# Masked pairs of v and r: one VectorE operation in place of a ScalarE copy and two GpSimd selections

## The chip, the cores and the metric

The kernel runs on one core of a Trainium2 chip. A core has a matrix engine (TensorE, in the profile PE, its weight loads PEld), a vector engine (VectorE, DVE), a scalar engine (ScalarE, ACT) and a general engine (GpSimd, POOL). DMA queues are fed by the sync engine (SP) and by ACT. Matmul results land in PSUM, eight banks of 2 KB per partition; everything else lives in SBUF. The metric is the device time of one execution in microseconds; lower is better. Before the change the median of three timed runs is 599.76 us (597.77 to 600.04).

## The reference

A recurrent attention with a 40 x 40 state per head (4 batches, 8 heads, 768 steps), followed by a small MoE-like product on its output. In short:

```python
# r, k, v, w, a, b: (4, 8, 768, 40) float32
for t in range(S):
    y[:, :, t] = einsum('bhd,bhde->bhe', rt, state)
    Sa = einsum('bhde,bhe->bhd', state, at)
    state = state * wt[:, :, None, :] - einsum('bhd,bhe->bhde', Sa, bt) \
            + einsum('bhd,bhe->bhde', vt, kt)
x = y.transpose(0, 2, 1, 3).reshape(B * S, H * D)      # (3072, 320)
a = x @ w1; b = x @ w2                                 # w1, w2: (320, 1024)
out = ((a * b) @ w3) @ w_out                           # w3: (1024, 1024), w_out: (1024, 320)
```

The weights of the MoE part arrive as 8-byte floats.

## The kernel before

**Tiling.** The 768 steps are cut into 12 chunks of 64 (C = 64). Inside a chunk the recurrence becomes matrix work: the steps of a chunk act on each other through a strictly triangular 64 x 64 matrix per head, which is inverted, and the state is carried from chunk to chunk. The eight heads of a batch are four pairs (NP = 4); the two heads of a pair sit in the two halves of the 128 partitions. Two batches are done together, so a chunk has two such groups.

**Stages of one chunk**, by the tags of the code: `ld` loads decay (fm), k and b (xx) and a (aa); `sc` scans the decay and scales aa and xx with it; `ca` forms the causal products (PSUM to JP and lm, lm masked by POOL); `so` inverts the triangular blocks in many small DVE operations (multiply into tmp, reduce, in lines 681 and 685); `jo` joins the blocks; `pa` forms the pair products of v and r; `tk` transposes xx into bk; `rec` (tags `r.`) runs the recurrence of the chunk on PE, with DVE masking (un, line 922) and ACT copies (un, hs, SB) between the products; `ga` gathers y into xr by DMA; `m.` is the MoE part: xs (xr split in a high and a low part, lines 972 and 975), products with w1 and w2 (line 988), a * b (ga, line 1001), its split in gh and gl (gl in line 1004), the output product (line 1013) and the store. w3 and w_out are multiplied once at the start (line 540) after their conversion from 8-byte floats (`cv`, lines 443 to 461), piece by piece through four raw buffers. A check of the weights (`ck`, lines 484 to 496) reads them a second time along the way.

**The pairs.** For each chunk and batch, `pa.mm` (line 822) writes a 128 x 256 product into a PSUM bank. An ACT copy `pa.cp` (line 827) brings it into vg, columns 0 to 63 of each pair; then two POOL selections `pa.mask` (line 831), one for each half of the partitions, set to zero what is not strictly above the diagonal. The other 40 columns of each pair come by DMA (`pa.v`). The recurrence reads vg in `r.zv` and in two more products. This is done 48 times (12 chunks x 4 batches).

**What sets the order.** Every step is recorded as an operation with a tag, its reads and its writes. The table RANK gives each operation a number, and the whole program is written out in the order of these numbers; each engine works through its operations in that order. The table ON says for seven kinds of operation, one letter per instance, which engine does it (d DVE, p POOL, a ACT). Buffers are handed out in the same order: a slot is free again when its last reader has been written out. One rule concerns DVE and POOL: DVE operations whose tag is in the set TWO are noted, and a POOL operation is given a dependence on the last noted one ahead of it in the program. The pair copies, as well as the other operations that read PSUM (un, y, st, a * b), are not in that set.

**The mask.** mask_h is made at the start: -1 where the column is greater than the row of its half, 0 elsewhere in the first 64 columns, and -1 in the other 40. The masking of un multiplies a PSUM bank with it.

## Time and profile before

| | |
|---|---|
| median of 3 timed runs | 599.76 us |
| profiled execution | 603.52 us |
| its span, first to last instruction | 601.8 us |
| PE busy | 544.7 us, 91% |
| DVE busy | 496.2 us, 82% |
| ACT busy | 411.9 us, 68% |
| POOL busy | 149.1 us, 25% |
| mean granted PE clock | 0.978 |

A busy time is a union over the engine's instructions, as a share of the span. Idle time of PE is what its instructions waited for others. The profiled execution is a single one; its time is compared with its own span, and the median stands for the kernel.

### The profile page before, as it was taken

The numbers are of one execution on the slowest core, as the hardware profiler recorded it, in microseconds if no ns is written. First come the engines' busy times: TensorE is split into PE (matmuls) and PEld (weight loads), VectorE is DVE, ScalarE is ACT, GpSimd is POOL, SyncE is SP. The second block draws the span as 40 slices with busy tenths as digits, with TensorE's granted clock in tenths as the row PEclk, the third lists the DMA queues.
The fourth block names the chain that finished last, engine by engine and source line by source line (L and its number), as shares of the span: only waits on it lengthen the run. The fifth ranks groups of instructions, "written<-read, shape, count | busy, mean of one in ns | idle before, by whom it ended". The sixth has DMA issues, their size and how long they took to land.

```text
span 601.8 us, 26711 instructions
## 1 busy us (share of the span) xinstructions
PE 544.7 (91%) x11714; PEld 491.4 (82%) x11714; DVE 496.2 (82%) x955; ACT 411.9 (68%) x888; POOL 149.1 (25%) x218
## 2 busy tenths in 40 slices
PE   1197998899999999999999899999999999999994
PEld 1175676799888898899898798998988998998994
DVE  5998899899699797995797896995997998956672
ACT  7888859954947649548639549567576497377562
POOL 3013242112411324034322133233121330151000
PEclk9997999799999999999999999998998999999998
DMA  8988785442235053533252535334452445337671
GB/s 249 295 274 261 223 244 144 114 126 52 77 100 151 18 146 90 136 85 98 52 165 62 132 83 148 98 80 127 131 137 90 145 123 167 107 96 225 225 242 30
DMA packets 56812, 83.45 MB, mean 139 GB/s; under 512 B 30320, under 2 KB 38000, under 8 KB 56688
## 3 DMA queue, kind: packets, MB, share of 16 engines
q1 hardware_dynamic: 56300, 81.34, 47.8%
q8 instruction: 94, 1.54, 1.1%
q10 hardware_dynamic: 388, 0.33, 0.2%
q14 instruction: 30, 0.25, 0.1%
HBM read 72.99 MB, written 3.93 MB: 128 GB/s over the span
## 4 chain that ended last, share of the span: by engine, by line
PE 56%; DVE 21%; ACT 12%; issue 5%; DMA 4%; SPq 1%; ACTq 0%; POOL 0%; DVEq 0%
PE bank L988 24%; PE bank L871 15%; PE bank L1013 9%; DVE tmp L681 4%; ACT JP L330 3%; PE bank L629 3%; ACT TT L330 2%; DVE TDX L657 2%; PE bank L846 2%; DMA fm<-in_fmg_dram 2%; PE bank L822 1%; PE bank L783 1%; DVE Tp L685 1%; DVE un L922 1%; DVE TDX L685 1%
## 5 line engine op out<-in xcount | busy, mean ns | idle before, releaser
L988 PE MATMUL bank<-xs,W 128*128 128x256 f32 x1536 | 208.4, 288 | 1.2 <-ACT ga L330 0.6
L988 PEld LDWEIGHTS bank<-xs,W 128*128 128x128 f32 x1536 | 189.8, 190 | 9.1 <-issue 1.5
L1004 POOL TENSOR_TENSOR gl<-ga,gh 128x512 fp32r<-128x512 f32 x30 | 38.6, 1288 | 145.1 <-DVE tmp L681 49.8
L831 POOL TENSOR_SCALAR_AFFINE_SELECT vg<-vg 64x256 f32<-64x256 f32 x96 | 42.4, 448 | 117.8 <-DVE tmp L681 48.5
L1013 PE MATMUL bank<-W3h,gh 128*128 128x320 f32 x192 | 62.3, 324 | 0.0
L1013 PE MATMUL bank<-W3h,gl 128*128 128x320 f32 x192 | 59.6, 310 | 0.6 <-POOL gl L1004 0.6
L1013 PE MATMUL bank<-W3l,gh 128*128 128x320 f32 x192 | 59.3, 309 | 0.0
L330 ACT ACTIVATE ga<-bank 128x512 f32<-128x512 f32 x48 | 28.4, 597 | 42.4 <-PE bank L988 42.2
L645 POOL TENSOR_SCALAR_AFFINE_SELECT lm<-lm 64x512 f32<-64x512 f32 x48 | 33.4, 701 | 86.9 <-DVE tmp L681 30.4
L871 PE MATMUL bank<-un,bk 64*64 64x104 f32 (+1 forms) x768 | 46.2, 258 | 5.6 <-DVE un L922 5.5
L330 ACT ACTIVATE JP<-bank 64x256 f32<-64x256 f32 (+2 forms) x120 | 45.2, 378 | 7.1 <-PE bank L629 4.7
L871 PE MATMUL bank<-hs,TT 64*64 64x104 f32 x768 | 47.1, 263 | 1.3 <-ACT TT L330 1.2
L330 ACT ACTIVATE gh<-ga 128x512 fp32r<-128x512 f32 x48 | 30.3, 631 | 25.5 <-DVE ga L1001 22.7
L871 PEld LDWEIGHTS bank<-un,bk 64*64 64x64 f32 (+1 forms) x768 | 36.4, 126 | 12.3 <-DVE un L922 8.5
L1001 DVE TENSOR_TENSOR ga<-bank,ga 128x512 f32<-128x512 f32 x48 | 32.9, 686 | 15.7 <-ACT ga L330 7.9
L871 PE MATMUL bank<-vg,bk 64*40 64x104 f32 (+1 forms) x768 | 44.9, 256 | 0.7 <-issue 0.7
L846 PE MATMUL bank<-ident,xx 104*128 104x104 f32 x192 | 27.4, 273 | 18.3 <-DVE xx L601 18.3
L922 DVE TENSOR_TENSOR un<-bank,mask_h 128x416 f32<-128x416 f32 x48 | 28.2, 587 | 18.4 <-PE bank L871 16.4
L629 PE MATMUL bank<-aa,xx 40*64 40x64 f32 x1536 | 32.2, 237 | 10.5 <-DVE aa L590 7.3
L871 PEld LDWEIGHTS bank<-hs,TT 64*64 64x64 f32 x768 | 37.2, 138 | 4.7 <-ACT TT L330 1.7
L540 PE MATMUL bank<-wof,w3f 128*128 128x320 f32 x128 | 40.6, 471 | 0.0
L629 PEld LDWEIGHTS bank<-aa,xx 40*64 40x64 f32 x1536 | 29.1, 150 | 14.0 <-issue 10.5
(127 smaller groups left out, 1265.0 us busy)
## 6 DMA issues: line engine op xcount, KB each, us to landing
rv<-in_rv_dram SPq DMA_DIRECT2D x24, 588.0 KB
xx<-in_fmx_dram SPq DMA_DIRECT2D x24, 448.0 KB
raw<-in_w3t_dram SPq DMA_DIRECT2D x16, 512.0 KB
JP<-in_w3t_dram SPq DMA_DIRECT2D x11, 512.0 KB
fm<-in_fmg_dram SPq DMA_DIRECT2D x24, 227.5 KB
aa<-in_fma_dram SPq DMA_DIRECT2D x24, 224.0 KB
raw<-in_w_dram SPq DMA_DIRECT2D x10, 512.0 KB
vg<-in_vt_dram SPq DMA_DIRECT2D x48, 80.0 KB
```

Of the source, the lines that this page charges most:

```text
L330: act.activation(out_, in_, AF.Copy, scale=scale)
L540: pe.matmul(out=pt.t[:, 0:DM], lhsT=w[:, j], rhs=wof[:, j], start=(j == 0), stop=(j == NJ - 1))
L629: pe.matmul(out=bank(s)[64 * z:64 * z + 64, i, p], lhsT=X[r, p, z], rhs=aa.t[r, i, p], start=True, stop=True)
L645: op("ca.mask", lambda q=q: pool.affine_select(out=lm.t[q], in_=lm.t[q], pattern=[[0, 2 * NP], [1, C]], compare_op=ALU.is_gt, fill=0.0, ba ...
L831: op("pa.mask", lambda q=q, vg=vg: pool.affine_select(out=vg.t[q, :, 0:C], in_=vg.t[q, :, 0:C], pattern=[[0, NP], [1, C]], compare_op=ALU. ...
L846: pe.transpose(out=bank()[:, p], in_=X[:, p].rearrange("q x t -> q (x t)"), identity=ident[0:104, 0:104])
L871: pe.matmul(out=out_(ab ^ z, p), lhsT=left(ab, ab ^ x, p), rhs=right(ab ^ x, p), start=start and p == 0, stop=True, skip_group_check=True)
L922: dve.tensor_tensor(out=un[i].t, in0=view(hp[i]), in1=mask_h.unsqueeze(1).to_broadcast([128, NP, N]), op=ALU.mult)
L988: pe.matmul(out=pt.t[:, TOK * x:TOK * x + TOK], lhsT=WT[k][:, cs], rhs=xs.t[:, z], start=(n == 0), stop=(n == 7))
L1001: op("m.ab", lambda a=a, pt=pt: dve.tensor_tensor(out=a.t, in0=wide(pt), in1=a.t, op=ALU.mult), r=[pt], w=[a])
L1004: both("m.gl", lambda e, a=a, j=j: e.tensor_tensor(out=gl.t[:, j:j + 2], in0=a.t, in1=gh.t[:, j:j + 2], op=ALU.subtract), r=[a, (gh, j)], ...
L1013: pe.matmul(out=pt.t[:, 0:DM], lhsT=l.t[:, j, ts], rhs=W3[r][:, j], start=(j == 0 and n == 0), stop=(j == NJ - 1 and n == 2))
```

## The change

The pair products leave PSUM in one DVE operation: out = (PSUM * -1) * mask_h. Since the mask holds -1 and 0, this is the copy and the selection at once, for all 128 partitions. The ACT copy and the two POOL selections go. All tables of the order (RANK) and of the engines (ON) are replaced. In ON the count of DVE instances changes for gl (18 to 8 of 48), aa (15 to 13 of 24), xx (20 to 16 of 24), the conversion sums cv.add (26 to 23 of 31) and the check's squarings ck.sq (18 to 13 of 31); in the first four the rest is on POOL, in the last on ACT. Line numbers behind the tables move by 4, and behind the edited lines by 8.

```diff
 OPS = {
...
-    "act": "... jo.cp1 jo.cp2 jo.tt pa.cp tk.cp r.n "
+    "act": "... jo.cp1 jo.cp2 jo.tt tk.cp r.n "
-    "dve": "cv.t cv.add/d ...
+    "dve": "pa.cp cv.t cv.add/d ...
-    "pool": "w.lo/p cv.add/p sc.aa/p sc.xs/p ca.mask pa.mask m.gl/p",
+    "pool": "w.lo/p cv.add/p sc.aa/p sc.xs/p ca.mask m.gl/p",
...
 ON = {
-    "cv.sign": "aadaaddaadadaaaaddaaaaaadaadaaa",
-    "cv.add": "dddddddpdddddddddddpdpddddpdpdd",
-    "w.lo": "dddpddpddddp",
-    "sc.aa": "ddddddddpdpppddppdpdpdpd",
-    "sc.xs": "ddddddpddddddppdddpddddd",
-    "m.gl": "ddddppppppdpdpdpdpppddpppdpdpppdpppdpppppppdddpd",
-    "ck.sq": "ddaaaaaaddddaddadddaadaadddddda",
+    "cv.sign": "aaaaadadaaddaaaadaaaaaadddaaada",
+    "cv.add": "dpdddddddpdddddddddppppdpdpdddd",
+    "w.lo": "ddppdddddpdd",
+    "sc.aa": "ddpdpdpppdddpdpdpdppdddp",
+    "sc.xs": "ddddpdpppdddpdpdddpdpddd",
+    "m.gl": "pddppppdpppppppppppppppppdpppppppppppppppdppdpdd",
+    "ck.sq": "ddaaddaadaaaaadaadadaddaadaadad",
 }
...
-    "pa.cp": "135 140 211 216 333 348 416 403 638 627 697 708 ...
+    "pa.cp": "250 267 277 275 321 325 421 445 643 623 699 698 ...
...
         for vg, pt in zip(vgs, pts):
-            op("pa.cp", lambda vg=vg, pt=pt: copy(vg.t[:, :, 0:C], bank(pt)[:, :, 0:C]), r=[pt],
-               w=[(vg, 0), (vg, 1)])
-            for ab in range(2):
-                q = slice(64 * ab, 64 * ab + 64)
-                op("pa.mask", lambda q=q, vg=vg: pool.affine_select(
-                    out=vg.t[q, :, 0:C], in_=vg.t[q, :, 0:C], pattern=[[0, NP], [1, C]], compare_op=ALU.is_gt, fill=0.0,
-                    base=0, channel_multiplier=-1), w=[(vg, ab)])
+            op("pa.cp", lambda vg=vg, pt=pt: dve.scalar_tensor_tensor(
+                out=vg.t[:, :, 0:C], in0=bank(pt)[:, :, 0:C], scalar=-1.0,
+                in1=mask_h[:, 0:C].unsqueeze(1).to_broadcast([128, NP, C]), op0=ALU.mult, op1=ALU.mult), r=[pt], w=[(vg, 0), (vg, 1)])
```

On DVE, ahead of the inversion of the second chunk (the transposition of JP into TDX), the order before reads as follows; ISA is a sum of the weight conversion (line 461).

```order
105 L461 ISA mf_170<-mf_170,rs_169 128x1024
106 L461 ISA w3f_177<-w3f_177,rs_168 128x1024
107 L447 TENSOR_SCALAR mf_171<-raw_164 128x512
108 L657 STREAM_TRANSPOSE TDX_121<-JP_145 128x32x32
109 L681 TENSOR_TENSOR tmp<-DG,TDX_121 128x4
```

At the same place the order now holds the first chunk's four evacuations of the pairs (line 823), between conversion steps:

```order
103 L457 ISA w3f_177<-w3f_177,rs_168 128x1024
104 L450 TENSOR_SCALAR rs_168<-raw_163 128x512
105 L443 TENSOR_SCALAR mf_170<-raw_163 128x512
106 L823 SCALAR_TENSOR_TENSOR vg_126<-bank_153,mask_h 128x4x64
107 L457 ISA mf_170<-mf_170,rs_168 128x1024
108 L823 SCALAR_TENSOR_TENSOR vg_127<-bank_155,mask_h 128x4x64
109 L823 SCALAR_TENSOR_TENSOR vg_124<-bank_157,mask_h 128x4x64
110 L653 STREAM_TRANSPOSE TDX_121<-JP_145 128x32x32
111 L677 TENSOR_TENSOR tmp<-DG,TDX_121 128x4
```

Three of the four are seen here, the fourth stands a few rows further up. On POOL, in the same early part of the program, the order before reads (line 831 is a selection on vg, line 645 one on lm, line 461 a conversion sum):

```order
35 L645 AFFINE_SELECT lm_118<-lm_118 64x512
36 L831 AFFINE_SELECT vg_127<-vg_127 64x4x64
37 L831 AFFINE_SELECT vg_126<-vg_126 64x4x64
38 L645 AFFINE_SELECT lm_117<-lm_117 64x512
39 L461 TENSOR_TENSOR w3f_177<-w3f_177,rs_168 128x512
40 L461 TENSOR_TENSOR w3f_178<-w3f_178,rs_169 128x512
41 L461 TENSOR_TENSOR mf_170<-mf_170,rs_168 128x512
```

And now:

```order
31 L641 AFFINE_SELECT lm_117<-lm_117 64x512
32 L457 TENSOR_TENSOR w3f_179<-w3f_179,rs_169 128x512
33 L641 AFFINE_SELECT lm_118<-lm_118 64x512
34 L457 TENSOR_TENSOR w3f_178<-w3f_178,rs_168 128x512
35 L457 TENSOR_TENSOR w3f_177<-w3f_177,rs_169 128x512
36 L524 TENSOR_TENSOR W_2_103<-mf_171,W_0_102 128x512
37 L457 TENSOR_TENSOR w3f_178<-w3f_178,rs_168 128x512
```

The selections on vg are gone and conversion sums stand in their place. On ACT, at the end of the program, the gather of the last chunk (DMA into xr) and the split of its result (xs) read before as follows; the lines 484 and 490 are steps of the weight check.

```order
709 L947 DMA xr_143<-y_142 40x256
710 L484 ACTIVATE JP_145<-JP_145,half 128x512
711 L947 DMA xr_143<-y_142 40x256
712 L947 DMA xr_143<-y_142 32x256
713 L484 ACTIVATE JP_144<-JP_144,half 128x512
714 L947 DMA xr_143<-y_142 8x256
715 L947 DMA xr_143<-y_142 32x256
716 L330 ACTIVATE gh_1646<-ga_1650 128x512
717 L330 ACTIVATE ga_1649<-bank_153 128x512
718 L484 ACTIVATE TDX_121<-TDX_121,half 128x512
719 L490 ACTIVATE TDX_121<-TDX_121,middle 128x512
720 L330 ACTIVATE gh_1646<-ga_1649 128x512
```

And now:

```order
659 L939 DMA xr_143<-y_142 8x256
660 L326 ACTIVATE ga_1614<-bank_153 128x512
661 L939 DMA xr_143<-y_142 32x256
662 L480 ACTIVATE JP_144<-JP_144,half 128x512
663 L939 DMA xr_143<-y_142 40x256
664 L326 ACTIVATE gh_1610<-ga_1613 128x512
665 L939 DMA xr_143<-y_142 8x256
666 L480 ACTIVATE TDX_121<-TDX_121,half 128x512
667 L326 ACTIVATE gh_1610<-ga_1614 128x512
668 L486 ACTIVATE TDX_121<-TDX_121,middle 128x512
669 L480 ACTIVATE JP_145<-JP_145,half 128x512
670 L964 ACTIVATE xs_1612,stats<-xr_143 128x768
```

Three gather issues now stand together ahead of these rows, the first steps of gh stand between the later ones, and fewer check steps are left between them. On PE, behind the last recurrence product and ahead of the last chunk's MoE products, 48 MoE and 48 output matmuls stood before; now it is 32 and 48.

## Rows read from the trace of the kernel before

**Rows 1.** The page, part 1: busy us (share of the span) and instructions of each engine.

```profile
PE 544.7 (91%) x11714; PEld 491.4 (82%) x11714; DVE 496.2 (82%) x955; ACT 411.9 (68%) x888; POOL 149.1 (25%) x218
```

**Rows 2.** Stages: length, busy us of PE, PEld, DVE, ACT, POOL; PE clock, DMA, GB/s.

```profile
0.00:120.57 120.57, 86.05 (x1929) 65.88 (x1929) 105.47 (x205) 99.81 (x202) 28.91 (x55) 0.94 0.78 225
120.57:550.00 429.43, 414.97 (x9329) 383.51 (x9328) 362.06 (x687) 284.75 (x643) 116.31 (x160) 0.99 0.41 111
550.00:601.80 51.80, 43.65 (x463) 41.97 (x458) 28.70 (x64) 27.35 (x45) 3.89 (x3) 0.95 0.54 170
```

**Rows 3.** Chain of waits: start us, us, what; first and last chunk's first MoE matmuls.

```profile
120.57 2.26 PE bank L988 x16
...
571.80 14.29 PE bank L988 x120
```

**Rows 4.** What PE waited for from 120 to 550 us: total, times, longest.

```profile
PE bank L871 <- DVE un L922: 3.1, 6, 0.8
...
PE bank L629 <- ACT xs L972: 1.7, 2, 1.0
PE bank L783 <- DVE TDX L734: 1.7, 4, 0.9
...
PE bank L988 <- ACT ga L330: 0.6, 1, 0.6
PE bank L871 <- POOL vg L831: 0.6, 2, 0.4
...
```

**Rows 5.** Groups of instructions: busy us, mean ns, idle before; the removed copy and selections.

```profile
L330 ACT ACTIVATE vg<-bank 128x256 f32<-128x256 f32 x48 | 17.7, 380 | 10.6 <-PE bank L822 10.5
...
L831 POOL TENSOR_SCALAR_AFFINE_SELECT vg<-vg 64x256 f32<-64x256 f32 x96 | 42.4, 448 | 117.8 <-DVE tmp L681 48.5 <-DVE xx L601 16.6 <-DVE aa L590 16.2
```

**Rows 6.** Groups of instructions on DVE nearest to the new operation.

```profile
L922 DVE TENSOR_TENSOR un<-bank,mask_h 128x416 f32<-128x416 f32 x48 | 28.2, 587 | 18.4 <-PE bank L871 16.4 <-ACT hs L330 1.2 <-ACT W L330 0.3
...
L931 DVE TENSOR_TENSOR y<-bank,fm 104x256 f32<-104x256 f32 x48 | 19.3, 414 | 0.5 <-PE bank L871 0.5
L597 DVE SCALAR_TENSOR_TENSOR gi<-gt,gi 104x512 f32<-104x512 f32 x24 | 16.5, 688 | 0.7
```

**Rows 7.** Groups of instructions that change their engine, on DVE and (gl) on POOL.

```profile
L601 DVE TENSOR_TENSOR xx<-xx,gi 104x1024 f32<-104x1024 f32 x20 | 24.9, 1245 | 1.1 <-DMA xx<-in_fmx_dram 0.9
...
L1004 DVE TENSOR_TENSOR gl<-ga,gh 128x512 fp32r<-128x512 f32 x18 | 12.3, 685 | 3.3 <-ACT gh L330 3.1
...
L590 DVE TENSOR_TENSOR aa<-aa,fm 104x512 f32<-104x512 f32 x15 | 10.2, 683 | 1.2 <-DMA aa<-in_fma_dram 1.2
...
L461 DVE CUSTOM_DVE_ANT_0 w3f<-w3f,rs 128x1024 uint16<-128x1024 uint16 x14 | 9.4, 678 | 0.0
...
L492 DVE SCALAR_TENSOR_TENSOR JP<-JP 128x512 f32<-128x512 f32 x12 | 8.5, 710 | 3.6 <-ACT JP L484 3.6
...
L1004 POOL TENSOR_TENSOR gl<-ga,gh 128x512 fp32r<-128x512 f32 x30 | 38.6, 1288 | 145.1 <-DVE tmp L681 49.8 <-ACT gh L330 46.7 <-ACT SB L330 17.0
```

**Rows 8.** In order of time: the last weight piece's issue, and its first step on DVE.

```profile
85.65 0.38 SPq L444 DMA_DIRECT2D raw<-in_w_dram  x1
...
111.30 0.42 DVE L447 TENSOR_SCALAR mf<-raw 128x512 int32<-128x512 int32 x1
```

**Rows 9.** In order of time, last stage: PE and DVE behind the last recurrence product.

```profile
557.82 4.07 PE L988 MATMUL bank<-xs,W 128*128 128x256 f32 x32
...
568.16 0.42 PE L1013 MATMUL bank<-W3h,gl 128*128 128x320 f32 x1 [0.55 <-POOL gl L1004]
...
570.06 0.96 DVE L975 TENSOR_TENSOR xs<-xr,xs 128x768 fp32r<-128x768 f32 x1
```

## The prediction

> **What bounds the kernel now.** I read the totals first, then the busy time by stage, then who TensorE (PE) waits for, and last the durations of the operations that the change touches. PE is busy 544.7 us of a span of 601.8; VectorE (DVE) 496.2, ScalarE (ACT) 411.9 [rows 1]. PE's own work stays as it is, so the time is that work plus PE's idle time, and I look for where the 57.1 idle us (601.8 minus 544.7) lie. By stage [rows 2]: up to 120.57 us PE is busy 86.05, so 34.5 idle; from there to 550 it is busy 414.97 of 429.43, 14.5 idle; behind 550 43.65 of 51.8, 8.15 idle. The first mark is the start of the first matmul of the MoE stage [rows 3], from which PE always has independent work at hand.

> In the first stage DVE is busy 105.47 of 120.57 and ACT 99.81 [rows 2]: weight conversion, scaling, the first two block inversions and the first recurrence all stand in DVE's queue, and PE waits for DVE. This stage is bound by DVE, with ACT close behind. In the middle stage PE is 97% busy (414.97/429.43), and what it waits for by name is small: 4.8 us for DVE (un 3.1, TDX 1.7), 2.3 for ACT (xs 1.7, ga 0.6) and 0.6 for the masked vg of GpSimd (POOL); the other eight rows of that answer name no engine or hold 0.5 us or less each [rows 4]. The 42.4 us that POOL spends on the masks therefore cost PE almost nothing today.

> **The change part by part.**

> Removed: 48 ACT copies of 380 ns (17.7 us) and 96 POOL selections of 448 ns (42.4 us) [rows 5]. ACT loses 17.7 us, less the five squarings of the weight check that it takes over; POOL loses 42.4 less what the new tables send there.

> Added: 48 DVE operations on 128x256, one operand in PSUM and one the mask in SBUF. The trace of before has no such row. The nearest are the y products, also PSUM times SBUF and 256 columns, at 414 ns, and the masking of un, with the same mask but 416 columns, at 587 ns; that the operation has two arithmetic steps adds nothing visible, since the three-operand form on 512 columns takes 688 ns against 685 for a plain difference of 512 columns [rows 6, 7]. Bounds 0.41 and 0.59; I take 0.42, nearest to the row with the same columns: 48 x 0.42 = 20.2 us on DVE.

> Moved between engines by the new tables (letters in the rows of the diff): on DVE ten fewer differences gl (10 x 0.685 = 6.9), two fewer aa products (2 x 0.683 = 1.4), four fewer xx products (4 x 1.245 = 5.0), three fewer conversion sums (3 x 0.678 = 2.0), five fewer squarings (5 x 0.71 = 3.6): 18.9 us [rows 7]. DVE thus ends 20.2 - 18.9 = 1.3 us heavier over the whole program. POOL takes the differences at 1288 ns each instead of 685 [rows 7], off PE's path as long as the output matmuls stand behind other work.

> First stage. PE has the same matmuls ahead of the first MoE matmul in both orders (counted in the order: 64 weight-product, 192 causal, 128 small-block, 128 join, 64 pair, 40 transpose, 368 recurrence), so its start follows from DVE. Ahead of the first low-part split (xs, line 975), which releases that matmul, DVE gains eight evacuations (8 x 0.42 = 3.4 us) and loses three conversion sums, two aa and one xx product (2.0 + 1.4 + 1.2 = 4.6 us): -1.2 us on an engine that is 87% busy there (105.47/120.57). By bounds: 8 x 0.59 = 4.7 would make it +0.1. ACT loses eight copies ahead of the same point (8 x 0.38 = 3.0 us), which is worth something only where DVE waits for ACT. Transfers: up to the last piece of the output weight the queue of SP carries one fm load of 227.5 KB more than before, and the very last weight piece now stands behind the gather of the first chunk. Before, that piece is issued at 85.65 and its conversion starts on DVE at 111.30 [rows 8], 25 us later, so I price both at nothing; the new place costs something only if the gather, and the piece behind it, is issued over 20 us later than that. I take -1.2, from -4.2 (ACT's 3.0 counts in full) to +3.4 (the evacuations count in full and what went to POOL is waited for).

> Middle stage. DVE gets the other 40 evacuations. In the new order one of the 48 stands directly ahead of an un masking, for which PE waits, and three within three places; so PE's wait for un grows by 3 x 0.42 = 1.3 us at most if only these delay it. Against this ACT is lighter, and of the 2.3 us that PE waits for it, plus 0.6 for vg, I count most as gone: -2.0. With +1.0 for un I take -1, between -2.9 (those waits all gone, nothing on un) and +4.8 (they stay, and DVE's 4.8 us double).

> Last stage. Behind the last recurrence product PE must bridge the gather of the last chunk until xs is split. Before, PE goes on at 557.82, the low part is there at 571.02 (570.06 + 0.96), and the last chunk's matmuls run from 571.8 [rows 3]; between them PE has 48 MoE and 48 output matmuls, with one stall of 0.55 us for gl [rows 9]. In the new order only 32 and 48 are left there; 32 MoE matmuls took 4.07 us [rows 9], so 16 fewer are 2.0 us less cover. The gap is not all paid: in the new ACT order three gather issues stand together, and only one weight-check step stands between them and the next, so the gather is issued sooner. I take +1.0, between 0 and +2.6 (2.0 plus a second stall of 0.55 or so).

> Sum: -1.2 - 1.0 + 1.0 = -1.2 us. The profiled execution took 603.52, its span 601.8 and 1.7 around it, so the sum says 602.3 for it; it lies 3.8 above the median of the three timed runs (599.76). Against that median: 598.6.

> **The rivals.**

> DVE becomes the limit (slower). The first stage hangs on DVE. If the sums, aa and xx products that went to POOL come late there (a sum takes POOL about twice as long as DVE, as gl does), DVE waits for them and what it gave up buys nothing, while the 8 evacuations still cost 3.4 us. With the last stage's +1.0: 599.76 + 3.4 + 1.0 = 604.2. It decides from the point where PE's first MoE matmul starts later than 123 us. For it: DVE is the busiest engine of that stage. Against it: POOL is busy only 28.91 of 120.57 us there [rows 2]. [...]

> ACT was the hidden limit (faster). In the first stage ACT is busy 83% (99.81/120.57), and chains there run from ACT to DVE and back. If its eight copies count in full, the first stage gives -4.2; if in the middle stage PE's named waits for ACT and POOL go, -2.9; with +1.0 at the end: 599.76 - 6.1 = 593.7. For it: ACT and POOL each lose work, and the chain from the pair product to vg becomes one operation for three. Against it: PE waited only 0.6 us for vg.

> Nothing is gained or lost (no change). PE is 97% busy in the long stage whatever feeds it, and the new order shifts small waits around: 599.8. The change would do what it says and be off the path. I keep it inside the forecast's own range.

> **How the numbers follow.** Forecast with the no-change case 0.56, ACT the hidden limit 0.25, DVE the limit 0.19. About 0.5% (3.0 us) is what a measurement of this kernel can tell from no change. The forecast's own range is 595 to 602.5; of its 0.56 about 0.10 lies under 596.8 and 0.02 above 602.8. The second case gives 0.24 to faster and 0.01 to same, the third 0.17 to slower and 0.02 to same. So faster 0.34, same 0.47, slower 0.19. The range from 592 to 605 takes in most of both rivals; the ends of all three stages together (-7.1 and +10.8) are taken in on the faster side, with 0.7 more for what no row names, and left out on the slower.

> **What would show it.** The new rows on DVE near 0.42 us; DVE's total near 497 to 498, ACT's down by about 14, gl on POOL 40 times. The first MoE matmul starts between 116 and 124 us. PE's idle time in the middle stage stays between 10 and 18 us. Behind the last recurrence product PE shows a new wait for xs of about 1 us. Wrong would be: evacuations near 0.6 us, a first MoE matmul that moves by over 4 us, or a new wait of PE for vg or gl of several us in the middle.

## The result, and the profile after

The changed kernel took 603.77 us (median of 16 runs, 598.41 to 611.43) against 600.00 for the kernel before on the same chip (16 runs, 596.35 to 602.73). The ratio is 1.0057, 95% interval 1.0031 to 1.0082: 0.57% slower, some 3.4 us. The time lies inside the forecast range, but the forecast (598.6, no change or slightly faster) has the wrong sign. A ratio here leaves out runs over 1.5% above the fastest of their kernel, a median holds all runs.

The profiled execution took 606.24 us, its span 604.5; that of the kernel before, 603.52, lies above all 16 of its timed runs. So the two profiles show where two single executions differ, and not by how much the medians do. The totals after answer to [rows 1]:

```profile
PE 545.9 (90%) x11714; PEld 493.7 (82%) x11714; DVE 495.7 (82%) x979; ACT 403.2 (67%) x845; POOL 135.4 (22%) x141
```

The new operation and its neighbours, from the groups of instructions (busy us, mean ns of one, idle before), answer to [rows 6] and the last row of [rows 7]:

```profile
L823 DVE SCALAR_TENSOR_TENSOR vg<-bank,mask_h 128x256 f32<-128x256 f32 x48 | 19.0, 409 | 0.1
...
L914 DVE TENSOR_TENSOR un<-bank,mask_h 128x416 f32<-128x416 f32 x48 | 28.1, 585 | 18.6 <-PE bank L863 18.4
...
L996 POOL TENSOR_TENSOR gl<-ga,gh 128x512 fp32r<-128x512 f32 x40 | 51.6, 1290 | 251.0 <-DVE tmp L677 110.4 <-ACT gh L326 59.7 <-DVE JP L492 20.0
```

The stages, cut at the first MoE matmul and at the end of the last recurrence product (columns as in [rows 2]); first the kernel after, then the same cut in the kernel before, whose first stage is the first row of [rows 2]:

```profile
0.00:119.64 119.64, 86.43 (x1930) 66.83 (x1931) 106.91 (x209) 97.06 (x193) 30.14 (x47) 0.93 0.76 224
119.64:561.72 442.08, 425.60 (x9529) 393.83 (x9528) 369.46 (x726) 283.80 (x618) 101.37 (x92) 0.98 0.42 113
561.72:604.50 42.78, 33.85 (x262) 33.03 (x258) 19.31 (x45) 22.32 (x36) 3.90 (x3) 0.95 0.52 160
```

```profile
120.57:557.82 437.25, 422.79 (x9513) 390.36 (x9513) 367.58 (x699) 290.95 (x654) 117.61 (x161) 0.99 0.41 112
557.82:601.80 43.98, 35.83 (x278) 35.13 (x274) 23.18 (x52) 21.15 (x35) 2.59 (x2) 0.94 0.52 164
```

The order after has 16 MoE matmuls more ahead of the second cut (32 instead of 48 behind it), which is 2.0 us of work. So the first stage is 0.9 us shorter, the middle stage 442.08 - 2.0 - 437.25 = 2.8 longer, the last stage 42.78 + 2.0 - 43.98 = 0.8 longer: together the 2.7 us between the spans. In this pair the loss is in the middle stage. Of the 2.8 us 2.0 are idle time of PE (16.5 against 14.5); the rest is PE's own work, which took 425.60 - 2.0 - 422.79 = 0.8 us longer for the same matmuls. PE's waits there, which answer to [rows 4] (total, times, longest):

```profile
PE bank L863 <- DVE un L914: 4.3, 4, 1.9
PE bank L863 <- issue: 3.4, 4, 2.2
PE bank L779 <- ACT JP L326: 1.5, 1, 1.5
PE bank L863 <- ACT un L326: 1.4, 2, 0.8
PE bank L779 <- issue: 1.1, 1, 1.1
...
PE bank L980 <- DVE vg L823: 0.6, 1, 0.6
```

Two things stand out. The wait for un reaches 1.9 us, and a wait of 2.2 us has no releaser ("issue": nothing that the profile shows ended it). In order of time on PE, around the latter:

```profile
371.00 0.91 PE L863 MATMUL bank<-vg,lm 64*64 64x104 f32 x29
374.08 0.30 PE L863 MATMUL bank<-vg,lm 64*64 64x104 f32 x2 [2.17 <-issue]
...
376.58 2.08 PE L980 MATMUL bank<-xs,W 128*128 128x256 f32 x8
...
380.18 2.07 PE L980 MATMUL bank<-xs,W 128*128 128x256 f32 x8
```

PE stops after 29 of 32 matmuls of one product. These need nothing that the first 29 did not need. Behind it eight MoE matmuls take 2.08 us; in E8 below, at the same place, 1.22. In stretches (columns as above; the last three are granted clock, DMA share, GB/s):

```profile
366.00:368.00 2.00, 2.00 (x19) 2.00 (x18) 1.38 (x2) 1.95 (x6) 0.00 (x0) 1.00 0.74 195
368.00:370.00 2.00, 1.96 (x81) 1.65 (x83) 1.82 (x3) 1.95 (x6) 0.00 (x0) 1.00 1.04 303
370.00:372.00 2.00, 1.91 (x96) 1.72 (x87) 1.97 (x5) 1.94 (x5) 0.00 (x0) 1.00 0.96 334
372.00:374.00 2.00, 0.00 (x0) 0.00 (x0) 1.46 (x2) 1.60 (x3) 0.21 (x1) 1.00 0.17 54
...
378.00:384.00 6.00, 6.00 (x107) 5.30 (x106) 2.02 (x6) 2.55 (x6) 0.00 (x0) 0.50 0.68 202
```

The granted clock, 1.00 up to the end of the stall, is 0.50 from 378 to 384 us, with PE busy for all 6.00 us. Ahead of the stall the DMA engines are full (a share of 0.96 to 1.04) and PE runs 81 and 96 matmuls in 2 us each. The transfers issued just before (loads, and the stores of `out_dram`):

```profile
365.48 0.35 SPq L479 DMA_DIRECT2D TDX<-in_w_dram  x1
365.93 1.16 SPq L1014 DMA_DIRECT2D out_dram<-o  x2
367.14 0.57 SPq L559 DMA_DIRECT2D xx<-in_fmx_dram  x1
367.76 0.48 SPq L479 DMA_DIRECT2D JP<-in_w_dram  x1
```

That is 512 + 160 + 448 + 512 KB within 2.8 us. And the DMA queues of the last microsecond before the stall (packets, MB, share):

```profile
q1 hardware_dynamic: 110, 0.35, 96.5%
q8 instruction: 1, 0.02, 6.7%
```

That such waits are waits for instructions is argued from all 16 profiles. Between 120 and 560 us PE has 104 waits of over 0.15 us without a releaser; every one of them ends 2.2 to 3.3 us after a packet of q8 starts. Of the 280 waits with a releaser 59 do.

The other wait, for un at 462.66, has a different history. The rows are from DVE, where the operation ahead of the masking waited 1.76 us for ACT:

```profile
461.42 0.69 DVE L488 SCALAR_TENSOR_TENSOR TDX<-TDX 128x512 f32<-128x512 f32 x1 [1.76 <-ACT TDX L480]
462.02 0.58 DVE L914 TENSOR_TENSOR un<-bank,mask_h 128x416 f32<-128x416 f32 x1
```

ACT in its turn waited for a load of the weight check, issued at 454.58 and used from 460.64. PE lost 1.85 us, and in the same way 1.83 at 549.36 (behind the check) and 1.48 at 233.14 (behind a late fm load on ACT).

The last stage, in order of time on PE, answers to [rows 9]; no wait for xs is named:

```profile
561.72 4.04 PE L980 MATMUL bank<-xs,W 128*128 128x256 f32 x32
...
569.97 0.41 PE L1005 MATMUL bank<-W3h,gh 128*128 128x320 f32 x1 [0.69 <-ACT gh L326]
571.33 0.41 PE L1005 MATMUL bank<-W3h,gl 128*128 128x320 f32 x1 [0.81 <-POOL gl L996]
```

### The profile page after: what moved, and what is told of

Read it like the earlier page. It is cut to its first block, busy times and chain, and to the rows that moved or that the text cites. A ratio compares the mean times of both kernels' runs of the same rounds, so it can differ in the third digit from the quotient of the medians.

```text
span 604.5 us, 26628 instructions
## 1 busy us (share of the span) xinstructions
PE 545.9 (90%) x11714; PEld 493.7 (82%) x11714; DVE 495.7 (82%) x979; ACT 403.2 (67%) x845; POOL 135.4 (22%) x141
## 4 chain that ended last, share of the span: by engine, by line
PE 60%; DVE 17%; ACT 8%; DMA 6%; issue 4%; SPq 3%; POOL 1%; ACTq 0%; DVEq 0%; POOLq 0%
PE bank L980 25%; PE bank L863 14%; PE bank L1005 10%; DVE tmp L677 3%; PE bank L536 3%; PE bank L625 3%; DMA TDX<-in_w3t_dram 2%; ACT JP L326 2%; PE bank L779 2%; PE bank L838 2%; SPq L939 2%; DVE TDX L653 2%; DMA rv<-in_rv_dram 2%; DMA fm<-in_fmg_dram 1%; DVE un L914 1%
## 5 line engine op out<-in xcount | busy, mean ns | idle before, releaser
L996 POOL TENSOR_TENSOR gl<-ga,gh 128x512 fp32r<-128x512 f32 x40 | 51.6, 1290 | 251.0 <-DVE tmp L677 110.4
L863 PE MATMUL bank<-vg,bk 64*64 64x104 f32 (+1 forms) x768 | 46.5, 259 | 1.2 <-issue 1.2
L326 ACT ACTIVATE JP<-bank 32x256 f32<-32x256 f32 (+2 forms) x120 | 45.4, 379 | 2.9 <-PE bank L625 0.9
L993 DVE TENSOR_TENSOR ga<-bank,ga 128x512 f32<-128x512 f32 x48 | 32.8, 685 | 16.7 <-PE bank L980 10.9
L326 ACT ACTIVATE bk<-bank 128x416 f32<-128x416 f32 x48 | 24.3, 513 | 24.9 <-PE bank L838 24.8
L677 DVE TENSOR_TENSOR tmp<-Tp,TDX 128x256 f32<-128x256 f32 (+2 forms) x57 | 39.2, 687 | 0.9
## 6 DMA issues: line engine op xcount, KB each, us to landing
fm<-in_fmg_dram SPq DMA_DIRECT2D x24, 227.5 KB
```

Of the source, the lines that this page charges most:

```text
L326: act.activation(out_, in_, AF.Copy, scale=scale)
L677: dve.tensor_tensor(out=scratch(*shape), in0=x().to_broadcast([128, *shape]), in1=y().to_broadcast([128, *shape]), op=ALU.mult)
L863: pe.matmul(out=out_(ab ^ z, p), lhsT=left(ab, ab ^ x, p), rhs=right(ab ^ x, p), start=start and p == 0, stop=True, skip_group_check=True)
L993: op("m.ab", lambda a=a, pt=pt: dve.tensor_tensor(out=a.t, in0=wide(pt), in1=a.t, op=ALU.mult), r=[pt], w=[a])
L996: both("m.gl", lambda e, a=a, j=j: e.tensor_tensor(out=gl.t[:, j:j + 2], in0=a.t, in1=gh.t[:, j:j + 2], op=ALU.subtract), r=[a, (gh, j)], ...
```

## The experiments

E1 to E4 shared a chip and the runs of the kernel before there; so did E5 to E8, E9 to E11, and E13 and E14. The changed kernel itself has ratios of 1.0057, 1.0141 and 1.0056 in its three groups of runs, so runs are best compared beside each other.

| run | kernel | median us (runs) | ratio to before, 95% interval |
|---|---|---|---|
| E1 | operation alone, old order | 609.43 (6) | 1.0174, 1.0135 to 1.0213 |
| E2 | new tables alone, old operations | 615.92 (6) | 1.0291, 1.0254 to 1.0328 |
| E3 | changed, late loads unblocked | 609.64 (6) | 1.0104, 1.0042 to 1.0166 |
| E4 | changed | 606.93 (6) | 1.0141, 1.0106 to 1.0176 |
| E5 | changed, one load moved | 603.38 (12) | 0.9998, 0.9957 to 1.0039 |
| E6 | changed, E3 and three loads moved | 599.43 (12) | 0.9995, 0.9965 to 1.0024 |
| E7 | operation and new letters, old order | 632.72 (6) | 1.0530, 1.0485 to 1.0574 |
| E8 | changed | 603.54 (12) | 1.0056, 1.0023 to 1.0088 |
| E9 | changed, three loads moved | 598.66 (12) | 0.9996, 0.9966 to 1.0026 |
| E10 | E6 and four steps of the last stage | 601.42 (12) | 1.0028, 0.9996 to 1.0059 |
| E11 | E6 again | 601.13 (12) | 1.0007, 0.9972 to 1.0042 |
| E12 | before, one load moved into a burst | 598.70 (12) | 0.9990, 0.9962 to 1.0018 |
| E13 | E12, and a MoE group moved | 602.04 (12) | 1.0017, 0.9973 to 1.0061 |
| E14 | before, the MoE group moved | 603.14 (12) | 1.0044, 1.0006 to 1.0082 |

**E1: is it the operation or the tables?**

```diff
 (kernel before, RANK and ON unchanged)
-            op("pa.cp", lambda vg=vg, pt=pt: copy(...
-                op("pa.mask", ...
+            op("pa.cp", lambda vg=vg, pt=pt: dve.scalar_tensor_tensor(...
```

> The operation alone: the masked pairs leave PSUM by one VectorE operation at the place of the old ScalarE copy, the two selections are gone, and the order and engine tables stay those of before. Theory T (the new tables cost the time: in-order engines stand behind loads that land late): 600 us as before, within 597.5 to 601.5, and no PE wait for un over 1 us in the middle stage. Rival O (48 operations of 0.41 us more on VectorE cost the time): 602.5 to 605, with PE's waits for un and xx up by several us and VectorE busy 515 us.

1.7% slower, beyond either range: theory T, which put all of the loss on the tables, falls in this form. The operation does cost where it is dropped into the old order. The cost is not in the first stage (first MoE matmul at 120.92) but in the middle: the last recurrence product ends at 568.23 instead of 557.82 (in a profiled execution of 614.21, the slowest of the six). PE's waits there:

```profile
PE bank L783 <- DVE TDX L734: 4.2, 6, 1.3
...
PE bank L1009 <- POOL gl L1000: 1.4, 3, 0.8
...
PE bank L1009 <- DVE vg L827: 0.9, 1, 0.9
...
PE bank L842 <- DVE vg L827: 0.7, 1, 0.7
```

TDX grew from 1.7 us [rows 4] to 4.2, and vg, now DVE's, is waited for by name.

**E2: the tables alone.**

```diff
 (changed kernel, copy and affine_select as before)
+RANK["pa.mask"] = [n + 0.3 + 0.3 * ab for n in RANK["pa.cp"] for ab in range(2)]
```

> The new tables alone: ScalarE copy and two GpSimd selections as before, at the place that the new tables give to the new operation. Theory T: 603 to 606 us, with the un waits of 1.8 us behind the weight check still there. Rival O: back at 599 to 601 us.

2.9% slower, worse than either theory said. The new tables have no place for the two selections; the run puts them directly behind the copy, which is a choice of this run. The new tables have no room for the old operations, as the old ones have none for the new. Tables and operation can't be priced apart and added: 1.7% and 2.9% alone, 0.6% together.

**E3: the late loads.**

```diff
+RANK["ck.abs"][14], RANK["ck.sq"][14], RANK["ck.max"][11] = 2217.3, 2217.6, 2643.5
+RANK["sc.max"][11], RANK["sc.scan"][11] = 1111.3, 1111.6
```

> The changed kernel with five steps moved by a few places, so that three waits for a late load no longer stand ahead of what PE needs: the weight check's steps on piece 14 and its maximum on piece 11 go behind the next masking of un, and the first step of one chunk's scan goes behind the copies of JP. Theory T: the three waits of PE (1.85, 1.83 and 1.48 us, 5.2 in all) go, less what is late next: 599 to 601.5 us. Rival O: 603 to 604.5, since nothing of the operation changes. [...]

The three named waits went (PE waited 0.4 us for un of DVE in the middle stage). The time did not fall to T's 599 to 601.5, which would be a ratio of at most 1.0031; it can't be told from that of E4 beside it. Theory T falls. Another reading is that the unnamed stall and the stretch at a clock of 0.50 behind it make the difference. The profiled execution has 9.1 us of unnamed stalls in the recurrence products, among them 3.00 at the same three matmuls; but at 613.46 it is the slowest of the six, and doesn't stand for E3.

**E4 and E8: the changed kernel again.**

> The changed kernel once more, for a second profile beside the three others on one chip. Theory T: 603 to 604.5 us, and the waits of PE for un of 1.8 us at the same two places. [...]

> The changed kernel again, as the yardstick of the three others on the same chip: 603 to 608 us, with the unnamed stall of some 2.2 us at the same instructions near 372 us in its profile, as in the two profiles before.

The stall comes back at the same instruction, vg,lm behind matmul 29 of 32. E4, then E8, in order of time on PE:

```profile
370.82 0.43 PE L863 MATMUL bank<-vg,lm 64*64 64x104 f32 x2 [2.17 <-issue]
```

```profile
375.32 0.30 PE L863 MATMUL bank<-vg,lm 64*64 64x104 f32 x2 [2.72 <-issue]
```

In both the instruction packet starts with none left. The clock behind it is 0.50 for some 10 us in E4, and stays 1.00 in E8. The un wait at 460 us is there in E4 (1.77, while ACT waits 1.89 for the load) and gone in E8, where ACT doesn't wait for it: it comes and goes with the landing of a load. The one at 549 us is gone in both, so T's "same two places" fails, and E4's median lies above T's range.

E4's profiled execution took 600.05 us, the least of its six and as much as the kernel before, with the stall, the lower clock and the un wait all in it. So these three don't make an execution slow by themselves. The middle stages of E4 and E8:

```profile
117.25:555.73 438.48, 425.32 (x9529) 392.96 (x9527) 369.87 (x724) 282.88 (x616) 101.24 (x92) 0.99 0.42 114
```

```profile
119.54:558.63 439.09, 424.27 (x9528) 391.67 (x9528) 370.36 (x726) 283.70 (x618) 101.26 (x92) 0.99 0.41 113
```

Less the 2.0 us of added matmuls, three profiles of the changed kernel give 440.1, 436.5 and 437.1 against 437.25 before: single profiles scatter by as much as the loss. Chance decides part of the loss, which fits the wide spread of the runs (598.41 to 611.43, where before had 596.35 to 602.73).

**E5, E6, E9: the loads.**

```diff
 E5  +RANK["ck.in"][9], RANK["ck.abs"][9] = 1812.5, 1850.5
 E9  = E5, +RANK["ck.in"][6], RANK["ck.in"][10] = 2069.5, 2207.5
 E6  = E9 and the moves of E3
```

Theory F is that the late packet of instructions makes the loss: behind loads that fill the DMA engines (a share of 0.96 to 1.04 in the first profile) it starts with no instructions left, PE stands still (2.17 us there), and the clock behind the stall is lower (0.50). If it holds, E5 takes that stall away, for 3 to 6 us less than the changed kernel beside it.

> The changed kernel with one load of the weight check (piece 9, 512 KB) issued some 10 us later, behind a burst of loads, and its first step moved accordingly. [...] Rival N (the stall has nothing to do with the loads): the stall stays, and the time is that of the changed kernel within 1 us.

> The changed kernel with the five moves of the third run and the loads taken out of three bursts (pieces 9, 6 and 10 of the weight check issued behind the burst). Theory F with T: the waits behind late loads and the unnamed stalls near 372, 436 and 467 us both go, 5 to 9 us less than the changed kernel beside it, at or below the kernel before (597 to 600 us). Rival N: as the third run, no better than the changed kernel.

> The changed kernel with only the three loads moved (pieces 9, 6 and 10 of the weight check, taken out of the bursts near 367, 427 and 455 us), the steps that wait for late loads left where they are. If the late instruction fetch is the larger part of the loss (theory F): 600 to 601.5 us, most of what all eight moves gave. If only both together help: 602 to 604, as the changed kernel.

Beside each other on one chip stand E8 (1.0056) and E6 (0.9995): the three loads of 512 KB, issued later, together with the moves of E3, give back the loss (4.1 us by the medians, under the 5 to 9 expected). E3's moves alone had not. E9 has the loads alone, on another chip, and is no worse: 0.9996, where E6 repeated beside it (E11) has 1.0007. In one profile each, the middle stage of E6 is 3.0 us shorter than that of E8, and its last stage 2.7 longer (45.08 against 42.37):

```profile
119.28:555.32 436.04, 422.28 (x9529) 390.22 (x9528) 369.16 (x724) 283.07 (x617) 101.21 (x92) 1.00 0.41 114
```

In E9 the JP load is gone from the burst and stands at 379.66, as the SP queue of E9 shows:

```profile
368.22 0.35 SPq L481 DMA_DIRECT2D TDX<-in_w_dram  x1
...
369.88 0.57 SPq L561 DMA_DIRECT2D xx<-in_fmx_dram  x1
...
379.66 0.42 SPq L481 DMA_DIRECT2D JP<-in_w_dram  x1
```

The stall of E9 at these matmuls, and the ten microseconds behind it in the view of stretches:

```profile
375.83 0.30 PE L865 MATMUL bank<-vg,lm 64*64 64x104 f32 x2 [1.18 <-issue]
```

```profile
376.00:386.00 10.00, 10.00 (x247) 9.19 (x245) 9.62 (x26) 5.01 (x13) 1.29 (x1) 1.00 0.57 161
```

With the load moved the packet starts with 88 to 114 left in five profiles of five (E5, E6, E9, E10, E11), the stall there is 0.88 to 1.18 us, and the clock stays at 1.00. Without the move it starts with none in five of five (the first profile, E2, E3, E4, E8), and the stall is 2.17 to 3.00. E5's time is inconclusive: its median is that of E8 (603.38, 603.54), its ratio is that of before (0.9998), and its runs spread from 595.29 to 607.03. Moving one load mends one stall; two others, at 429.80 (1.59) and 459.10 (1.95), stood in its profile.

**E7: the letters in the old order.**

```diff
 (E1, with the ON table of the changed kernel)
```

> The operation with the new letters (which take ten gl, two aa, four xx and three conversion sums to GpSimd and five squarings to ScalarE), in the old order. If what the operation costs under the old order (some 10 us) is VectorE's 20 us of added load, the letters give most of it back: 600 to 604 us. If it is the place of the evacuations in the old order (PE waiting for vg and for what stands behind it), they give little back: 606 to 610 us.

5.3% slower, the opposite of giving back, and beyond both ranges. The first MoE matmul starts at 131.16; PE waits for GpSimd by name in the first stage:

```profile
PE bank L629 <- POOL aa L590: 3.4, 2, 2.4
```

**E10, E11: the last stage.**

```diff
 (E6)
+RANK["ga2"][4], RANK["ck.abs"][21], RANK["m.xh"][11] = 2719.5, 2720.5, 2736.5
+RANK["m.ab"][43], RANK["m.gh"][43] = 2721.5, 2724.2
```

> All eight moves, and in the last stage four steps put ahead of a weight-check step that waits for its load: a * b and gh of the last tile but four, one gather, and the split of the last chunk. PE's two stalls there (1.18 for gh, 0.80 for gl) and the wait of the split behind the check go: 1 to 2 us under the run beside it without these four moves, and at or below the kernel before. If the split waits for the gather's landing and not for ScalarE's queue: no difference.

> The eight moves again, as the yardstick of the two others: 598.5 to 601 us, within 0.3% of the kernel before.

No gain (601.42 against 601.13): PE still stood 1.00 us for gh and 1.10 for gl. E11 is within 0.3% of before by its ratio, as expected; its median lies just above the range.

**E12 to E14: the stall made in the kernel before.**

```diff
 E12 +RANK["ld.xx"][18] = 1823.5
 E13 +RANK["ld.xx"][18], RANK["m.mm1"][100] = 1823.5, 1881.5
 E14 +RANK["m.mm1"][100] = 1881.5
```

Theory F in its first form, a burst alone, puts an unnamed stall of 1.5 to 3 us near 372 us into E12 (602 to 606 us in all). In its second, a burst and small matmuls without a pause together, it puts one of 0.5 to 2 us into E13 (600.5 to 605).

> The kernel before with one load moved: the 448 KB of xx for one chunk, issued near 342 us in its profile, now stand behind the two loads of the weight check issued near 366 and 368 us, as they do in the changed kernel. Nothing else moves, and the load's first reader comes 20 us later. [...]

> The kernel before with the load of the last run (xx moved into the burst near 367 us) and with one MoE group of eight matmuls, which stands between the recurrence products near 372 us, moved behind them, as in the changed kernel. [...] If the instruction fetch is not the cause: no unnamed stall there, 598 to 600.5 us.

> The kernel before with only the MoE group moved behind the recurrence products, the load where it was. Both theories: no stall of over 0.5 us with no named cause near 372 us, since the DMA engines have room for the fetch there: 598.5 to 601 us.

The stall near 372 us did not appear in any of them, and E12 (598.70) is no slower than before: theory F in its first form falls. The instructions left at the packet's start move as it says (166 before, 111 with the load in the burst, 168 with the MoE group moved, 93 with both) but don't reach zero. In E13 PE waits 1.49 us for un, until 375.51, while the packet that started at 373.31 is under way, which may cover what is left of a stall. A burst alone doesn't make the stall there; that taking a load out of it mends it is shown.

Two more things stand in these runs. E12 and E13 have such a stall elsewhere, at a place where the order of the kernel before is unchanged, E12's as follows (E13's is 1.75 at 289.97):

```profile
288.36 0.86 PE L989 MATMUL bank<-xs,W 128*128 128x256 f32 x5 [1.78 <-issue]
```

The packet there started with 6 and 7 left (135 before), behind a DMA share of 1.02 from 282 to 284 us in E12, and the clock from 290 to 296 us is 0.52 in E12 and 1.00 in E13. So the order before can run dry too, and E12 lost nothing by it. And E14 missed its range (598.5 to 601): one MoE group moved, with no load touched, cost 0.44% (0.06 to 0.82), nearly as much as the loss that is to be explained, without a stall of that kind near 372 us.

## Why the prediction was wrong

**The sum.** First stage -1.2 forecast, -0.9 in the profile (119.64 against 120.57): the size is right. The reason given, a lighter DVE, is not what the stage's rows show: DVE's busy time there rose from 105.47 to 106.91 us and ACT's fell from 99.81 to 97.06, so DVE waited less. Last stage +1.0 forecast, +0.8 measured: the size is right by luck, since the row is not. I expected a new wait for xs; PE waited 0.69 for gh and 0.81 for gl instead, ahead of the same matmuls. Middle stage -1.0 forecast, +2.8 measured in this pair: this is the step that failed. E4 and E8 show less there (436.5 and 437.1 against 437.25), but in them too the outer stages are about as forecast or better (first -3.3 and -1.0, last +0.6 and +0.4), and the loads that give the time back stand in the middle stage.

**Why the middle failed.** The step counted PE's named waits and took most of those for ACT and for vg as gone. They were not: PE waited 3.7 us for ACT in the middle stage before and 4.0 after, for other tiles (JP 1.5, un 1.4), and 0.6 for vg as before, now from DVE. The wait for un grew from 3.1 to 4.3, near the 1.0 allowed for it, though behind steps of the weight check and not behind the evacuations. And it put aside "the other eight rows of that answer", which name no engine or are small. Four of these rows are unnamed:

```profile
PE bank L783 <- issue: 1.9, 2, 1.3
PE bank L871 <- issue: 1.2, 3, 0.6
PE bank L629 <- issue: 0.9, 1, 0.9
PE bank L988 <- issue: 0.5, 1, 0.5
```

These 4.5 us were the sign that PE already ran out of instructions now and then: the four longest of these waits (1.27, 0.89, 0.59 and 0.57 us) begin at a count of 450, as those of the profile after do at 449 and 450. Their total hardly grew (4.7 after, 4.2 in E4, 6.1 in E8; 3.8 in E6, 3.4 in E9), so the stalls by themselves are not the loss. New tables move loads, as the prediction noted for the first stage, where it priced them at nothing; for the middle it did not look at them. There three loads of the weight check landed in bursts ahead of dense recurrence products, and moving them, with E3's moves beside E8 and alone in E9, gives the time of before.

The prediction also held that "PE's own work stays as it is". The clock says otherwise. On the chip of E8 the mean granted clock of the runs that the ratio counts is 0.9817 before and 0.9780 in E8, with mean times of 599.8 and 602.8; on that of E4 it is 0.9844 before and 0.9723, with 599.2 and 606.1. An estimate from this: some 545 us of PE work at a clock lower by 0.0037 take 2.0 us longer, and by 0.0121 6.6 us, which is two thirds of the one loss and nearly all of the other. In E6 the clock is back at 0.9798, by the same estimate 1.0 of the 2.8 us between E8 and E6. In E1 the clock (0.9818) accounts for 1.4 of 10.9 us; there the waits are the loss. How much of the changed kernel's loss is the stall, the lower clock behind it or the waits for late loads is split no further: E9's moves act on all three.

**The operation's price.** 0.42 us forecast, 0.409 measured, the lower bound. DVE's total 497 to 498 forecast, 495.7 measured. ACT's fall of 14 came out as 8.7 in the union of its busy time. The removed copies (17.7 us) and five squarings more (9 + 4 before, 12 + 6 after) are as counted; neighbours overlap in a union, so a sum of rows overstates what it loses. PE's idle time in the middle stayed within the 10 to 18 us named (16.5).

**The rivals.** DVE the limit: its 604.2 is close to the result, but by luck; by its own test it is not what happened, since the first MoE matmul came before 123 us. What it describes is E7, where the same letters stand in the old order. ACT the hidden limit: the waits it would take away were replaced, not removed. No change (599.8) is 4 us off; it holds for the changed kernel with three loads moved.

**What is shown and what is argued.** Shown: what operation and tables cost alone does not add up to what they cost together; in the new order the places of three loads give the loss back (E6 against E8, and E9 by its ratio), and the state of the instruction packet near 370 us goes with them (five profiles against five). Not shown: that these loads are what makes the new order slower than the old. The same moves were not tried in the old order, and E14 shows that another small move can cost 0.44%. Argued, with support from the traces: that the full DMA engines make a packet late. In the 16 profiles 937 packets between 120 and 560 us start behind 3 us with a DMA share under 0.8; 25 of them find 110 or fewer instructions left, one of these 10 or fewer. Behind a share of 0.95 or more start 105; 29 of them find 110 or fewer left, seven of these 10 or fewer. But the trace shows a packet's start and not its request, and E12 to E14 did not produce the stall where it was expected.

## What to carry to other kernels

A wait with no releaser in the middle of a group of matmuls is worth a look at the instruction queue: in this case all 104 of over 0.15 us in the long stage ended 2.2 to 3.3 us after a packet there, and the one behind a burst of loads, 2.17 to 3.00 us long, was 0.88 to 1.18 with one load issued later. When a change re-plans an order, compare where the large loads stand, not only the waits by name, and look at the granted clock of all runs. One profile on each side can't locate a loss of 0.6% where profiles of one kernel differ by as much. And a re-planned order belongs to the operations it was planned for; halves of such a change, measured alone, say little of the whole.

## What the runs showed of the hardware

Queue q8, of the kind "instruction", carried 94 packets of 16 KB, 256 of PE's instructions to each by the counts at PE's stops (449 and 450 over at the packets 57, 67 and 70 of the profile after), and the median packet started when some 200 were left (196 to 213 in 16 profiles). All 104 unnamed waits of PE of over 0.15 us between 120 and 560 us ended 2.2 to 3.3 us after such a start. Behind the burst of loads at 370 us (DMA share 0.96 to 1.04 in the first profile of the changed kernel) a packet started when none was left, in five profiles of five with this order of the loads, and PE stood 2.17 to 3.00 us.

Behind this stall the mean granted clock of ten microseconds was 0.50 in two profiles (the first, from 375 to 385 us, and E4), 0.66 in E3, 0.85 in E2 and 1.00 in E8, with the same recurrence products around it. Eight MoE matmuls took 1.22 us where the clock was 1.00 (E8, at 377.07) and 2.08 where it was 0.50 (the first profile, at 376.58).
